# Order of a normalising product, engine of two relus and shape of one weight load in a fused attention and gated-FFN kernel

## The chip, the cores and the metric

The kernel runs on one core of a Trainium2 chip. The metric is device time in microseconds (us) of one execution; lower is better. Where I say "the profile" of a kernel, it is one execution of it taken by the hardware profiler; each kernel has one.

## The reference, cut to what matters

```python
def _attn_ref(q, k, v, n_global, n_local):      # 4 batches, 8 heads, 768 positions, head size 64
    scores = scale * q @ k.T - slope * dist     # ALiBi bias, causal window of 96 and 8 global keys
    a = softmax(where(keep, scores, -1e9))
    return a @ v

def _moe_ref(x, w_gate, w_val, w_out):          # x: 3072 tokens x 512; inner width 1536
    return (relu(x @ w_gate) * (x @ w_val)) @ w_out
```

## The kernel before

Tokens are worked off in eight halves of 384. While TensorE does the FFN of one half, the attention of the next is woven in, in small pieces. In the FFN, a *gate* group is four matmuls whose sum lies in one bank of PSUM, the memory into which TensorE writes; a relu reads it and frees the bank. A *value* group is four more in another bank; VectorE multiplies it with the relu's result, which gives `ht` and frees that bank. Three banks go round:

```python
P["ff"] = ctx.enter_context(tc.tile_pool(name="ffps", bufs=3, space=bass.MemoryType.PSUM, ...))

def gate(fc):
    psg = P["ff"].tile([128, 512], FP32, name="ff_ps")
    ...                                              # four matmuls into psg
    if fc in by_vector:                              # two groups of the first half only
        nc.vector.tensor_scalar_max(gr, psg[:, 0:QH], 0.0)
    else:
        nc.scalar.activation(gr, psg[:, 0:QH], AF.Relu, bias=0.0, scale=1.0)

def val(fc):
    psv = P["ff"].tile([128, 512], FP32, name="ff_ps")
    ...                                              # four matmuls into psv
    nc.vector.tensor_tensor(ht[:, fc, :], psv[:, 0:QH], st[fc], op=ALU.mult)
```

The attention of a pair of heads ends with a logarithm and an exponential on ScalarE (together the reciprocal of the softmax sum) and with two products on VectorE, one per head, that normalise into `xT`, the input of the next FFN:

```python
if e == 1:                                           # second head of the pair
    nc.scalar.activation(rc, ln, AF.Exp, bias=0.0, scale=-1.0)
    for e_ in range(2):
        r = slice(64 * e_, 64 * e_ + 64)
        nc.vector.tensor_tensor(xT_of[s][r, p, :], av_of[s, p, e_][r, 0:QH], rc[r], op=ALU.mult)
```

Pieces and FFN groups are put in order by `weave`; each engine then executes its own instructions in that order. In the text, x0 and x1 are the two heads' products, "es" the mask products of the attention, and ht5 and ht6 are the two `ht` products near them. I count value groups from 0 to 95 over the program.

At the start, GpSimd issues the loads: the gate weights come as three transfers of 512 columns, and behind the first of them comes q and k of the second half:

```python
def load_gate(i):
    load_w(wg[i], moe_w_gate, i * GW * 128, (i + 1) * GW * 128)      # GW = 4
...
f1_0[0][1]()                 # the first two gate groups, ahead of the second half's attention
```

The softmax here doesn't subtract the row's maximum and nothing guards it: scores larger than these inputs give would overflow.

## Time and profile before

| | before |
|---|---|
| median of the first three runs | 253.26 us (252.5 to 254.62) |
| median of all six runs beside the changed kernel | 252.68 us (252.4 to 254.62) |
| span of the profiled execution | 251.0 us |
| TensorE busy, share of the span | 96% |
| stalls ahead of gate and value groups in the five later passes | 2.33 us |

A later pass is one half's FFN with the next half's attention woven in, some 28 us. Stalls are counted from start to start: a matmul of 384 columns takes 0.16 us, and what a step takes beyond that is a stall.

### The profile page before, as it was taken

Reading aid. Unit: us, or ns where it says so; the run is one execution under the profiler, and the core shown is the slowest. Engines: PE = TensorE matmul, PEld = TensorE weight load, DVE = VectorE, ACT = ScalarE, POOL = GpSimd, SP = SyncE. Lnnn points to the kernel's source line nnn. Section 1 sums busy time; section 2 is a strip of 40 time slices with the busy share of each in tenths; the row PEclk is TensorE's granted clock in tenths of the full one; section 3 lists DMA queues with packets and bytes.
Section 4 is the critical chain, followed back from the end, with each engine's and each line's share of the span. In section 5 each row is a group of like instructions: output and inputs, shape, how many; then the busy total and the mean of one; then the engine's idle time right before and its main releaser. Section 6 shows DMA issues by size and latency. Waiting matters only on the chain.

```text
span 251.0 us, 4966 instructions
## 1 busy us (share of the span) xinstructions
PE 240.0 (96%) x1779; PEld 141.9 (57%) x1789; DVE 133.6 (53%) x346; ACT 156.4 (62%) x316; POOL 94.0 (37%) x213
## 2 busy tenths in 40 slices
PE   7969999999999999999999999999999999999994
PEld 3646555556555666556664566556565566556543
DVE  3744854775465657527662557527662657524410
ACT  6878755337675787557774687557774687553312
POOL 7988929700557326803437066302440000000000
PEclk9999999999999999999999999999999999999999
DMA  6999999992799993978349956829541100020012
GB/s 189 150 180 159 182 200 103 142 178 56 246 138 257 159 222 90 126 136 267 83 108 89 252 149 158 59 103 274 87 105 58 70 0 1 3 102 24 0 44 84
DMA packets 77705, 31.57 MB, mean 126 GB/s; under 512 B 57585, under 2 KB 74737, under 8 KB 77681
## 3 DMA queue, kind: packets, MB, share of 16 engines
q0 software_dynamic: 36208, 9.48, 38.4%
q1 hardware_dynamic: 41472, 21.78, 33.1%
q8 instruction: 14, 0.23, 0.4%
q14 instruction: 11, 0.08, 0.1%
HBM read 28.38 MB, written 6.29 MB: 138 GB/s over the span
## 4 chain that ended last, share of the span: by engine, by line
PE 78%; DVE 6%; ACT 5%; DMA 4%; POOL 4%; issue 2%; POOLq 0%; ACTq 0%; DVEq 0%
PE ff_ps L545 24%; PE ff_ps L524 21%; PE ff_ps L511 21%; PE av_ps L423 5%; PE qk_ps L395 4%; DMA qs<-in_q_dram 3%; DVE ht L526 2%; DVE xT L440 2%; POOL vbuf L169 1%; PE av_ps L299 1%; ACT grelu L517 1%; ACT rcp L437 1%; ACT lnd L432 1%; ACT es L376 1%; DMA out_dram<-osb 1%
## 5 line engine op out<-in xcount | busy, mean ns | idle before, releaser
L524 PE MATMUL ff_ps<-xT,wv 128*128 128x384 bf16 x384 | 78.1, 326 | 1.4 <-DVE ht L526 0.4
L511 PE MATMUL ff_ps<-xT,wg 128*128 128x384 bf16 x376 | 76.5, 326 | 0.4 <-DVE ht L526 0.2
L517 ACT ACTIVATE grelu<-ff_ps 128x384 bf16<-128x384 f32 x92 | 45.0, 489 | 34.3 <-PE ff_ps L511 18.3
L526 DVE TENSOR_TENSOR ht<-ff_ps,grelu 128x384 bf16<-128x384 f32 x96 | 53.4, 557 | 23.5 <-PE ff_ps L524 17.9
L545 PE MATMUL ff_ps<-wo_sb,ht 128*128 128x512 bf16 x267 | 63.9, 379 | 0.5
L440 DVE TENSOR_TENSOR xT<-av_ps,rcp 64x384 bf16<-64x384 f32 x48 | 26.6, 555 | 44.8 <-ACT rcp L437 41.9
L524 PEld LDWEIGHTS <-wv 128*128 128x128 bf16 x384 | 36.1, 97 | 24.4 <-issue 3.2
L511 PEld LDWEIGHTS <-wg 128*128 128x128 bf16 x376 | 35.0, 97 | 23.0 <-issue 1.1
L407 DVE TENSOR_TENSOR es<-es,m_all 128x432 bf16<-128x432 bf16 (+5 forms) x108 | 33.1, 334 | 22.6 <-ACT es L398 22.1
L398 ACT ACTIVATE es<-qk_ps 128x432 bf16<-128x432 f32 (+2 forms) x72 | 37.9, 528 | 10.1 <-PE qk_ps L395 8.2
L545 PEld LDWEIGHTS <-ht 128*128 128x128 bf16 x276 | 25.8, 97 | 26.8
L313 POOL CAST kc<-ks 128x384 bf16<-128x384 f32 x20 | 10.0, 540 | 60.5 <-DMA ks<-in_k_dram 60.5
L432 ACT ACTIVATE lnd<-av_ps 64x384 f32<-64x384 f32 x48 | 23.3, 485 | 11.7 <-PE av_ps L423 11.0
L550 ACT COPY osb<-ff_ps 128x512 f32<-128x512 f32 x23 | 13.5, 585 | 23.3 <-PE ff_ps L545 22.5
L169 POOL DMA_DIRECT2D vbuf<-in_v_dram x28 | 24.3, 878 | 1.5 <-DMA qs<-in_q_dram 1.0
L395 PE MATMUL qk_ps<-qT,kT 128*128 128x432 bf16 (+5 forms) x108 | 24.8, 286 | 0.0
L423 PEld LDWEIGHTS <-vbuf 128*128 128x128 bf16 x216 | 18.0, 98 | 7.4
L423 PE MATMUL av_ps<-es,vbuf 128*128 128x216 bf16 (+4 forms) x216 | 21.0, 226 | 0.0
L395 PEld LDWEIGHTS <-kT 128*128 128x128 bf16 x108 | 10.6, 98 | 7.6
L321 POOL CAST qz<-qs 128x192 bf16<-128x192 f32 x40 | 12.6, 362 | 2.1 <-DMA qs<-in_q_dram 1.8
L437 ACT ACTIVATE rcp<-lnd 128x384 f32<-128x384 f32 x24 | 12.5, 522 | 0.8
L376 ACT ACTIVATE es<-qk_ps 128x864 bf16<-128x864 f32 (+3 forms) x16 | 10.4, 709 | 1.0 <-PE qk_ps L371 0.8
(85 smaller groups left out, 153.6 us busy)
## 6 DMA issues: line engine op xcount, KB each, us to landing
out_dram<-osb SPq DMA_DIRECT2D x23, 256.0 KB
ks<-in_k_dram SPq DMA_DIRECT2D x5, 768.0 KB
qs<-in_q_dram SPq DMA_DIRECT2D x5, 768.0 KB
vbuf<-in_v_dram POOLq DMA_DIRECT2D x24, 120.0 KB, 4.2
wg<-in_moe_w_gate_dram POOLq DMA_DIRECT2D x3, 512.0 KB, 7.5
wv<-in_moe_w_val_dram POOLq DMA_DIRECT2D x3, 512.0 KB, 9.3
wo_sb<-in_moe_w_out_dram POOLq DMA_DIRECT2D x1, 1536.0 KB, 12.5
ks<-in_k_dram SPq DMA_DIRECT2D x4, 192.0 KB
```

What stands on the lines that cost most here:

```text
L169: nc.gpsimd.dma_start(out=v_dst(b, NG + r0, NG + r0 + n, j), in_=v[b, :, KT * j + r0 : KT * j + r0 + n, :].rearrange("h p d -> p h d"))
L395: nc.tensor.matmul(ps[:, c : c + n_], lhsT=kt[:, j, :], rhs=qd[:, :, :, a : a + w], start=True, stop=True)
L398: nc.scalar.activation(es[:, 0:cols], ps[:, 0:cols], AF.Exp, bias=0.0, scale=scale)
L407: nc.vector.tensor_mul(e4, e4, mk)
L423: nc.tensor.matmul(av3[:, :, a : a + w], lhsT=vb[:, j, z0 : z0 + 128], rhs=es[:, c : c + NN * w].rearrange("k (n p) -> k n p", n=NN), star ...
L432: nc.scalar.activation(ln[o0 : o0 + 64], av[d0 : d0 + 64, 0:QH], AF.Ln, bias=0.0, scale=1.0)
L440: nc.vector.tensor_tensor(xT_of[s][r, p, :], av_of[s, p, e_][r, 0:QH], rc[r], op=ALU.mult)
L511: nc.tensor.matmul(psg[:, 0:QH], lhsT=w_of(wg, dc, fc), rhs=xT[:, dc, :], start=(dc == 0), stop=(dc == N_DC - 1))
L517: nc.scalar.activation(gr, psg[:, 0:QH], AF.Relu, bias=0.0, scale=1.0)
L524: nc.tensor.matmul(psv[:, 0:QH], lhsT=w_of(wv, dc, fc), rhs=xT[:, dc, :], start=(dc == 0), stop=(dc == N_DC - 1))
L526: nc.vector.tensor_tensor(ht[:, fc, :], psv[:, 0:QH], st[fc], op=ALU.mult)
L545: nc.tensor.matmul(ps2, lhsT=ht[:, fc, n * 128 : (n + 1) * 128], rhs=wo_sb[:, fc, :], start=(fc == 0), stop=(fc == N_FC - 1))
```

## The change

Its intent: after a reciprocal, an `ht` product that gives back a PSUM bank should not stand behind both heads' products; two relus should leave VectorE; and the first gates should start on half of the first gate columns, with the third gate group moved ahead of the second half's attention to fill the wait for q.

```diff
+    def load_first_gate():
+        for f0 in (0, GW * 64):
+            load_w(wg[0][:, :, f0 : f0 + GW * 64], moe_w_gate, f0, f0 + GW * 64)
...
-            for e_ in range(2):
-                r = slice(64 * e_, 64 * e_ + 64)
-                nc.vector.tensor_tensor(xT_of[s][r, p, :], av_of[s, p, e_][r, 0:QH], rc[r], op=ALU.mult)
+            av_of[s, p, "r"] = rc
+    def piece_x(s, p, e):
+        r = slice(64 * e, 64 * e + 64)
+        nc.vector.tensor_tensor(xT_of[s][r, p, :], av_of[s, p, e][r, 0:QH], av_of[s, p, "r"][r], op=ALU.mult)
...
-            return (T(0) + BI(0, 0, 1) + T(1) + f[8] + SC(0, 0, 1) + f[9] + T(2) + ...
+            return (T(0) + BI(0, 0, 1) + T(1) + SC(0, 0, 1) + f[8] + T(2) + ...
...
+        def with_x(item, p, e):                 # x0 in the piece that ends the pair, x1 in the next
+            return (item[0], lambda: (item[1](), piece_x(s, p, e)))
+        for p, at in ((0, 7), (1, 12), (2, 16), (3, 20)):
+            for e in range(2):
+                order[at + e] = with_x(order[at + e], p, e)
...
-            if fc in by_vector:
-                nc.vector.tensor_scalar_max(gr, psg[:, 0:QH], 0.0)
-            else:
-                nc.scalar.activation(gr, psg[:, 0:QH], AF.Relu, bias=0.0, scale=1.0)
+            nc.scalar.activation(gr, psg[:, 0:QH], AF.Relu, bias=0.0, scale=1.0)
...
     f1_0[0][1]()
+    f1_0[4][1]()                                # third gate group
```

More of the change, by code (lines that the diff above doesn't have):

```diff
@@ L437, in piece_av @@
             nc.scalar.activation(rc, ln, AF.Exp, bias=0.0, scale=-1.0)
-            for e_ in range(2):
-                r = slice(64 * e_, 64 * e_ + 64)
-                nc.vector.tensor_tensor(xT_of[s][r, p, :], av_of[s, p, e_][r, 0:QH], rc[r],
-                                        op=ALU.mult)
+            av_of[s, p, "r"] = rc
+    def piece_x(s, p, e):
+        r = slice(64 * e, 64 * e + 64)
+        nc.vector.tensor_tensor(xT_of[s][r, p, :], av_of[s, p, e][r, 0:QH], av_of[s, p, "r"][r], op=ALU.mult)
     def piece_av_wide(s, p):
@@ L479, in attention_pieces @@
             return (C(0) + X(lambda: load_v_globals(0), lambda: load_v(0, 0), lambda: load_v(0, 1),
-                             lambda: load_v(0, 2), lambda: load_v(0, 3), lambda: load_gate(0),
+                             lambda: load_v(0, 2), lambda: load_v(0, 3), load_first_gate,
                              lambda: load_qk_cast(1, 0, 2), lambda: load_qk_cast(1, 2, 4))
@@ L489, in attention_pieces @@
             f = [[x] for x in fill]
-            return (T(0) + BI(0, 0, 1) + T(1) + f[8] + SC(0, 0, 1) + f[9] + T(2) + BI(1, 0) + SC(1, 0) + BI(1, 1) + SC(1, 1)
+            return (T(0) + BI(0, 0, 1) + T(1) + SC(0, 0, 1) + f[8] + T(2) + BI(1, 0) + SC(1, 0) + BI(1, 1) + SC(1, 1)
                     + T(3) + SC(2, 0, 1) + f[0] + SC(3, 0) + f[1] + SC(3, 1) + f[2] + AW(0) + f[3] + AW(1) + f[4]
@@ L495, in attention_pieces, with ffn_pieces @@
         a = AV(2)
-        return (QK(0) + QK(1) + AV(0) + QK(2) + AV(1) + g[0:1] + a[0:1] + g[1:2] + a[1:2] + g[2:3]
-                + [(0.0, lambda: None)] * 2 + AV(3))
+        order = (QK(0) + QK(1) + AV(0) + QK(2) + AV(1) + g[0:1] + a[0:1] + g[1:2] + a[1:2] + g[2:3]
+                 + [(0.0, lambda: None)] + AV(3) + [(0.0, lambda: None)])
+        def with_x(item, p, e):
[3 more added lines that the diff above has]
+                order[at + e] = with_x(order[at + e], p, e)
+        return order
     out_v = out.rearrange("(s p n) d -> s n p d", p=128, n=NN)
-    def ffn_pieces(c, by_vector=()):
+    def ffn_pieces(c, pair_gates=False):
         ht = ht_pool.tile([128, N_FC, QH], BF16, name="ht")
@@ L566, in ffn_pieces @@
         f1 = []
-        if by_vector:
+        if pair_gates:
             f1 = [(0.65, two_gates), (0.65, lambda: val(0)), (0.0, lambda: None), (0.65, lambda: val(1))]
@@ L624 @@
     load_w(wo_sb, moe_w_out, 0, DM)
-    f1_0, f2_0 = ffn_pieces(0, range(GW, 2 * GW - 2))
+    f1_0, f2_0 = ffn_pieces(0, True)
     f1_1, f2_1 = ffn_pieces(1)
@@ L629 @@
     f1_0[0][1]()
+    f1_0[4][1]()
     for h in range(4, H):
         mask(h)
-    for _, f in attention_pieces(1, [f1_0[i] for i in (1, 3, 5, 7, 8, 10, 9, 11, 4, 6)]):
+    for _, f in attention_pieces(1, [f1_0[i] for i in (1, 3, 5, 7, 8, 10, 9, 11, 6)]):
         f()
```

## The prediction

> **What bounds the kernel now.** I read the page's busy shares first, then the busy time by stretches, then the waits of TensorE alone, then the chain of waits and the timeline where those waits lie.
>
> ```profile
> PE 240.0 (96%) x1779; PEld 141.9 (57%) x1789; DVE 133.6 (53%) x346; ACT 156.4 (62%) x316; POOL 94.0 (37%) x213
> ...
> 0.00:36.00 36.00, 30.33 (x397) 18.96 (x399) 21.28 (x70) 25.46 (x51) 29.08 (x58) 1.00 1.27 176
> ...
> 82.00:110.90 28.90, 28.46 (x193) 16.91 (x192) 16.70 (x41) 19.63 (x39) 12.52 (x30) 1.00 0.98 153
> 110.90:138.90 28.00, 27.73 (x182) 16.31 (x180) 15.41 (x36) 18.96 (x39) 11.72 (x29) 1.00 0.68 133
> ...
> PE ff_ps L560 <- DMA wg<-in_moe_w_gate_dram: 1.1, 1, 1.1
> PE av_ps L299 <- DMA qs<-in_q_dram: 1.0, 1, 1.0
> ...
> PE ff_ps L524 <- DVE grelu L515: 0.4, 1, 0.4
> ```
>
> The second to fourth lines are stretches (length, then busy time of TensorE matmul, weight load, VectorE, ScalarE, GpSimd). TensorE is the bound: 5.7 us of its 11 us of idleness lie in the first 36 us, and each later pass of about 28 us leaves 0.3 to 0.4 us. So nothing in this change can be worth much. TensorE's own work doesn't change; only its waits can. Busy time hides part of a wait, since the ends of matmuls are modelled. So I took the steps from start to start: four 128x384 matmuls take 0.65 us, that is 0.1625 us each, and what a step has beyond its own columns at that rate is a stall. Sums of this kind: 1.23 us ahead of the first gates (16.84), 1.13 us ahead of the second tile's transposes (19.27), five small ones from 25 to 40 us (0.31, 0.28, 0.53, 0.28, 0.24), and in the five passes with attention from 82 us on 0.72, 0.38, 0.54, 0.38, 0.31 us, 2.33 us together, all of them released by the product on L526.
>
> ```profile
> 9.67 0.80 POOL wg L186
> 10.46 0.69 POOL qs L145
> 11.15 8.07 DMA qs<-in_q_dram
> 19.23 0.04 issue
> 19.27 0.53 PE av_ps L299 x12
> ...
> 16.84 1.47 PE L560 MATMUL ff_ps<-xT,wg 128*128 128x384 bf16 x8 [1.05 <-DMA wg<-in_moe_w_gate_dram]
> 19.27 0.53 PE L299 MATMUL av_ps<-ident,qs 128*64 128x128 bf16 x12 [0.96 <-DMA qs<-in_q_dram]
> ```
>
> The chain passes through the gate load's issue and the q load behind it, not through the first gates: TensorE waits at 16.84 for the gate columns, but then waits again for q. Making the first wait shorter gains nothing unless work is moved into the second.
>
> ```profile
> 92.34 1.14 DVE L440 TENSOR_TENSOR xT<-av_ps,rcp 64x384 bf16<-64x384 f32 x2 [1.96 <-ACT rcp L437]
> 93.51 0.56 DVE L526 TENSOR_TENSOR ht<-ff_ps,grelu 128x384 bf16<-128x384 f32 x1
> 93.99 0.86 DVE L407 TENSOR_TENSOR es<-es,m_all 128x144 bf16<-128x144 bf16 x2
> 94.77 0.55 DVE L526 TENSOR_TENSOR ht<-ff_ps,grelu 128x384 bf16<-128x384 f32 x1
> ...
> 94.12 0.81 PE L524 MATMUL ff_ps<-xT,wv 128*128 128x384 bf16 x4
> ...
> 95.37 0.48 PE L511 MATMUL ff_ps<-xT,wg 128*128 128x384 bf16 x2 [0.25 <-DVE ht L526]
> ```
>
> VectorE sits idle 1.96 us behind the reciprocal, does both heads' products, and only then the product ht that gives a PSUM bank back. Call it ht5, and the next ht6. The value matmuls at 94.12 wait for ht5 (0.30 us), the gate at 95.37 for ht6 (0.42 us).
>
> **What the Trainium skill says.** "TensorE: Matmul & The Clock Gate", Architectural detail: ScalarE and VectorE take their queues strictly in order. The trace agrees: ht5's matmuls ended by 91.6, and it starts at 93.51, after both products. "VectorE: DVE Perf Modes", Two Vector instructions with no wait between them: an instruction whose inputs or output start in another group of 32 partitions than the one before is held until all earlier ones have finished. The trace agrees: the second head (partitions 64 up) starts 31 ns after the first has ended, ht5 32 ns after the second, while unheld neighbours start 80 ns before the end of the one before (0.474 us from ht5 to the es product, against 0.558 us long). "DMA: Bandwidth & Descriptors", Why a DMA increments its semaphore by 16 and not by 1: a load has landed only when all 16 engines have posted. In the trace's semaphore records 15 engines had posted the gate by 16.20 and the last at 16.79; for q of the first two heads it is 17.31 and 19.23. The slow engine also carried a 16 KB instruction fetch of 0.95 us from 17.02. "ScalarE: Activation LUTs", Rules for kernel authors, advises VectorE for a relu. Here, from PSUM, the trace has 548 ns on VectorE and 489 ns on ScalarE, so the move costs nothing.
>
> **The change part by part.**
>
> *Gate load in two.* One transfer of 1024-byte rows becomes two of 512-byte ones. At full rate the packet records show some 200 packets of 1024 bytes a microsecond and 480 of 384 bytes over 16 engines, so 80 and 33 ns an engine; on a straight line 512 bytes take 43 ns. An engine's 32 packets of 80 ns (2.56 us) become 64 of 43 (2.73 us): everything behind them in the queue lands about 0.2 us later, the q load at about 19.4 in place of 19.23. GpSimd pays one more issue, 0.8 us, which hides: the first k load is issued at 10.45 while its first packets move at 14.5. The first half lands, on the slowest engine, near 15 (half of its 12.86 to 16.79). TensorE is free at 15.8, so the first gates then wait for the last xT product, which ends at 17.21. They finish near 17.6 in place of 18.15. By itself that is worth nothing, for q still comes at 19.4.
>
> *Third gate moved ahead of the second tile.* This is what fills the hole. It needs a PSUM bank of the first gates, free after their relu at about 18.05, runs 18.1 to 18.75, and is done before q lands. The step that it leaves, between the transposes and the first scores, was 0.76 us (20.97 to 21.72 in the chain). From the transposes on, TensorE is therefore 0.76 - 0.2 = 0.55 us ahead. ScalarE follows: masks end near 21.2, and the first exponentials, now from 22.25, can start at about 21.4. The weights land early enough: the first value columns at 24.7 (+0.2) against use at 25.8 - 0.55, the second at 32.1 (+0.2) against 33.25 - 0.55.
>
> *Two relus to ScalarE.* The 0.53 us stall at 34.43 waits for the relu that VectorE ends at 34.39, behind a product. On ScalarE the first relu goes between the 0.52 us reciprocal that ends at 32.14 and the next logarithm, and the second follows 32.14 + 0.49 (relu) + 0.49 (ln) + 0.52 (exp) + 0.49, with issue gaps about 34.2. Gain 0.2 us. The 0.28 us stall at 37.49, behind a ScalarE relu, stays.
>
> *Second head's product one piece later.* The code spreads 22 pieces over 0.88 of 23.4 us, one per 0.94 us, between FFN groups of 0.65 us. Around the first pair the VectorE order is now x0, x1, ht5, es, es, ht6; it becomes x0, ht5, es, es, x1, ht6. So ht5 ends at 92.34 + 0.47 + 0.56 = 93.4 in place of 94.07, and the stall at 94.12 goes. But x1 still stands before ht6. VectorE is busy without a gap from 92.34 on, and there are two held starts before and after (x1 and ht5; then x1 and ht6). So ht6 still ends at about 95.3, and the gate at 95.37 waits for it just as long: 0.30 us is handed to the next wait. In the second kind of pass ht6 ends at 123.53 and the gate starts at 123.62, so some 0.05 us are won. Over five passes: about 0.1 us of the 2.33.
>
> That is so if the gate keeps the bank which ht6 frees. The bank freed by the relu at 94.02 is ready at 94.51. If the new order makes the allocation take that one, the waits vanish and all 2.33 us come back. In the kernel before, at this place the rotation already deviates: the gate at 93.17 waits for ScalarE and the value after it for VectorE, the reverse of the usual. I give this one chance in five.
>
> Sum: 0.55 + 0.2 + 0.1 = 0.85 us likely, 0.85 + 2.2 = 3.0 us at best; weighted 0.8 x 0.85 + 0.2 x 3.0 = 1.3 us. 253.26 - 1.3 = 252.0.
>
> **The rivals.** *The split delays q by more.* If 512-byte packets cost far more than the line says, or the instruction fetch and the slow engine add up worse, q lands 0.8 us later and eats the moved gate: gain 0.3 us or less, 253.0. For it: the slow engine is already 1.9 us behind the others at q. Against: the fetch is on that engine's path in both kernels. *All bank waits vanish*: about 250.3. For it: VectorE is 53% busy and idles 1.96 us just ahead. Against: the idle time lies before the burst, and the burst's length is unchanged. *Holding a PSUM bank longer hurts*: the second head's accumulator is released a piece later; but two more pieces pass before its next use, so I see no loss. *ScalarE becomes the bound*: 0.98 us more of 156.4 at 62%, no.
>
> **Range and chances.** Runs of the kernel before spread 252.5 to 254.62, so about 1 us is noise. The cases give 250.3 to 253.0; with noise 250.3 to 253.4. A gain of over 2% would need 5.1 us, most of the 6.3 us of all the stalls named above at once (1.23 + 1.13 + 1.64 + 2.33); a loss of that size has no source.
>
> **What would show it.** The first gates start near 15.8; the third gate's four matmuls lie before the second tile's transposes; those start at 19.3 to 19.7; no wait on a VectorE relu; x1 after the es products; the value matmuls near 93.5 no longer wait, and the gate two groups on still waits for L526 (or doesn't, in the rival with another bank). I am wrong if transposes start after 20.0, if all L526 waits are gone, or if a new wait appears after 36 us.

## More of the kernel before

The lines are in the prediction. One more, of the groups by line, is of use later. Its columns are line, engine, operation, tiles, shapes, count, then busy time and mean ns of one, then the engine's idle time ahead of the group and what ended most of it:

```profile
L440 DVE TENSOR_TENSOR xT<-av_ps,rcp 64x384 bf16<-64x384 f32 x48 | 26.6, 555 | 44.8 <-ACT rcp L437 41.9
```

VectorE idles 44.8 us in front of these products, nearly all of it for ScalarE's reciprocal: whatever stands behind the products in VectorE's queue waits with them.

## The result, and the profile after

The changed kernel took 250.12 us (median of six runs, 249.38 to 250.52) against 252.68 us. The ratio is 0.9885, with a 95% interval of 0.9854 to 0.9915. A ratio here is the mean time of one kernel's runs over that of the other's of the same rounds, so not quite the ratio of the medians. That is 1.2% faster: below the predicted range of 250.3 to 253.4 us.

To see where the time went I lined up the starts of the 96 value groups in the two profiles. TensorE's lead over the kernel before:

| value group (time before) | lead, us | what lies between |
|---|---|---|
| 0 (25.8 us) | 0.32 | start |
| 6 to 16 (36.6 to 52 us) | 0.87 | the two relus: +0.55 |
| 18 to 22 (55 to 61 us) | 0.26 | a new stall at 54 us: -0.61 |
| 24 (82.7 us) | 0.15 | -0.11, not traced |
| 32 | 0.86 | first later pass: +0.71 |
| 44 | 1.24 | second: +0.38 |
| 56 | 1.76 | third: +0.52 |
| 68 | 2.14 | fourth: +0.38 |
| 80 to 95 | 2.46 | fifth: +0.32 |

The steps sum to 0.32 + 0.55 - 0.61 - 0.11 + 2.31 = 2.46 us, and the spans differ by 251.0 - 248.5 = 2.5 us. The five passes gave all their stalls back; I had predicted 0.1 us there.

First the page's busy shares and groups of the profile after, then stretches of it (start:end, length, then busy time of TensorE matmul, weight load, VectorE, ScalarE and GpSimd, the granted clock, DMA share and GB/s):

```profile
PE 240.5 (97%) x1789; PEld 142.7 (57%) x1789; DVE 133.8 (54%) x344; ACT 157.2 (63%) x318; POOL 94.8 (38%) x214
...
L447 DVE TENSOR_TENSOR xT<-av_ps,rcp 64x384 bf16<-64x384 f32 x48 | 26.6, 555 | 35.2 <-ACT rcp L442 23.4
```

```profile
36.00:62.00 26.00, 25.43 (x190) 14.72 (x188) 16.83 (x45) 12.43 (x27) 10.76 (x17) 1.00 1.03 120
...
82.00:110.00 28.00, 28.00 (x193) 16.84 (x191) 16.37 (x40) 19.55 (x39) 12.26 (x30) 1.00 1.01 158
110.00:137.60 27.60, 27.60 (x182) 16.34 (x180) 15.57 (x36) 18.96 (x39) 11.73 (x29) 1.00 0.67 133
```

No engine does noticeably more or less work, and the products cost the same 555 ns each. But the idle time ahead of the products that is put down to the reciprocal has fallen from 41.9 to 23.4 us: work that stood behind both products now stands behind one. (It is not saved. The page puts 11.0 us ahead of the products down to the output matmuls, 2.2 us before, and VectorE's wait for ScalarE's es has grown from 22.1 to 30.1 us.) And in the passes from 82 us on TensorE is busy without a hole (28.00 of 28.00 us, 27.60 of 27.60 us). The stretch from 36 to 62 us, by contrast, has 0.57 us without work; that is the new stall.

The waits of TensorE (engine, tile and line, what it waited for, us in total, times, longest):

```profile
PE qk_ps L376 <- DVE kT L284: 0.7, 1, 0.7
PE ff_ps L523 <- ACT grelu L573: 0.4, 1, 0.4
PE ff_ps L523 <- DVE ht L535: 0.4, 1, 0.4
```

The line on the VectorE relu is gone. One wait on `ht` is left, and it is not in a later pass: it is the new one at 54 us. The second line is the moved third gate, waiting for the relu of the first gates.

Now the place from the prediction, 92 to 96 us, on VectorE and then on TensorE:

```profile
92.19 0.55 DVE L447 TENSOR_TENSOR xT<-av_ps,rcp 64x384 bf16<-64x384 f32 x1 [1.96 <-ACT rcp L442]
92.66 0.54 DVE L535 TENSOR_TENSOR ht<-ff_ps,grelu 128x384 bf16<-128x384 f32 x1
93.14 0.98 DVE L412 TENSOR_TENSOR es<-es,m_all 128x144 bf16<-128x144 bf16 x2
94.16 0.56 DVE L447 TENSOR_TENSOR xT<-av_ps,rcp 64x384 bf16<-64x384 f32 x1
94.75 0.56 DVE L535 TENSOR_TENSOR ht<-ff_ps,grelu 128x384 bf16<-128x384 f32 x1
```

```profile
93.67 0.81 PE L533 MATMUL ff_ps<-xT,wv 128*128 128x384 bf16 x4
...
94.50 0.81 PE L523 MATMUL ff_ps<-xT,wg 128*128 128x384 bf16 x4
```

The order is x0, ht5, es, es, x1, ht6, as predicted. ht5 ends at 93.20, so the value group at 93.67 doesn't wait. ht6 ends at 94.75 + 0.56 = 95.31, where I had said "about 95.3". Yet the gate group starts at 94.50, 0.8 us *before* ht6 ends. So it cannot be using the bank that ht6 frees.

The compiled programs say why. They list for each FFN tile its PSUM bank and the engine whose work its first matmul waits for. Around this gate (tile 70 in order of allocation, counted from 0; g and v are gate and value):

```
        before                      after
68 g    bank 6, waits for ScalarE   bank 6, waits for ScalarE
69 v    bank 7, waits for VectorE   bank 7, waits for VectorE
70 g    bank 5, waits for VectorE   bank 6, waits for ScalarE
71 v    bank 6, waits for ScalarE   bank 5, waits for VectorE
```

With the new order of instructions, tiles 70 and 71 have changed places: the gate got the bank that a relu on ScalarE frees, the value group after it the one that ht6 frees, and the value group comes 0.96 us later, at 95.46. Why the allocation picks so was not looked into; that it does is plain from the listing.

### The profile page after: what moved, and what is told of

It is laid out like the page before. It is cut to its first block, busy times and chain, and to the rows that moved or that the text cites. A ratio compares the mean times of both kernels' runs of the same rounds, so it can differ in the third digit from the quotient of the medians.

```text
span 248.5 us, 4970 instructions
## 1 busy us (share of the span) xinstructions
PE 240.5 (97%) x1789; PEld 142.7 (57%) x1789; DVE 133.8 (54%) x344; ACT 157.2 (63%) x318; POOL 94.8 (38%) x214
## 4 chain that ended last, share of the span: by engine, by line
PE 80%; DMA 8%; POOL 4%; DVE 3%; ACT 3%; issue 1%; SPq 1%; ACTq 0%; POOLq 0%
PE ff_ps L554 24%; PE ff_ps L523 21%; PE ff_ps L533 20%; PE av_ps L428 6%; PE qk_ps L400 5%; DMA wv<-in_moe_w_val_dram 5%; DMA qs<-in_q_dram 2%; POOL vbuf L169 1%; DVE qT L314 1%; PE qk_ps L358 1%; PE qk_ps L376 1%; DVE kT L282 1%; DMA out_dram<-osb 1%; POOL vbuf L174 1%; ACT lnd L469 1%
## 5 line engine op out<-in xcount | busy, mean ns | idle before, releaser
L526 ACT ACTIVATE grelu<-ff_ps 128x384 bf16<-128x384 f32 x94 | 45.9, 489 | 33.8 <-PE ff_ps L523 17.7
L535 DVE TENSOR_TENSOR ht<-ff_ps,grelu 128x384 bf16<-128x384 f32 x96 | 54.2, 566 | 22.5 <-PE ff_ps L533 19.0
L412 DVE TENSOR_TENSOR es<-es,m_all 128x432 bf16<-128x432 bf16 (+5 forms) x108 | 33.6, 339 | 30.4 <-ACT es L403 30.1
L447 DVE TENSOR_TENSOR xT<-av_ps,rcp 64x384 bf16<-64x384 f32 x48 | 26.6, 555 | 35.2 <-ACT rcp L442 23.4
L428 PE MATMUL av_ps<-es,vbuf 128*128 128x216 bf16 (+4 forms) x216 | 20.4, 226 | 0.0
```

The costliest lines, as they stand in the source:

```text
L412: nc.vector.tensor_mul(e4, e4, mk)
L428: nc.tensor.matmul(av3[:, :, a : a + w], lhsT=vb[:, j, z0 : z0 + 128], rhs=es[:, c : c + NN * w].rearrange("k (n p) -> k n p", n=NN), star ...
L447: nc.vector.tensor_tensor(xT_of[s][r, p, :], av_of[s, p, e][r, 0:QH], av_of[s, p, "r"][r], op=ALU.mult)
```

## The experiments

My theory after reading the result (A): the bank swap, which comes with the product's move, gives the five passes; the product's new place alone or the new banks alone would not. Rivals: (B) the order alone is enough, because VectorE has room; (C) the banks alone are enough; (D) the relus or the start gave a part of it. All kernels gave correct results.

### The parts of the change alone

**The product's move alone:**

```diff
-            for e_ in range(2):
...
-                nc.vector.tensor_tensor(xT_of[s][r, p, :], av_of[s, p, e_][r, 0:QH], rc[r], op=ALU.mult)
+            av_of[s, p, "r"] = rc            # and piece_x, with_x and the new order as in the change
```

> Only the second head's product is moved. Theory A (the passes' gain comes from the moved product together with the new PSUM bank that the allocation gives the gate behind it): the five stalls behind L526 in the passes vanish, 2.3 us, so about 250.4 where the kernel before has 252.7 (ratio 0.991), and no new stall near 54 us, since the start is not shifted. Rival B (my prediction as it stood, with the bank unchanged): 0.1 us, 252.6. Rival C (the gain is mostly the start's): under 1 us, above 251.7.

It took 251.05 us (250.31 to 251.72) against 252.87 us, ratio 0.9932 (0.991 to 0.9955), that is 1.7 us less, though I had expected 2.3; the reason comes below. In its profile no gate or value group of the later passes stalls, and the lead gained there is 2.30 us. Its compiled program has the changed kernel's bank map.

**The start's two parts alone:**

```diff
-                             lambda: load_v(0, 2), lambda: load_v(0, 3), lambda: load_gate(0),
+                             lambda: load_v(0, 2), lambda: load_v(0, 3), load_first_gate,
...
     f1_0[0][1]()
+    f1_0[4][1]()                            # and the list of fill pieces without it
```

> Only the gate load in two and the third gate moved ahead; relus and product as before. If the trace of the changed kernel reads true: TensorE is 0.3 us ahead from the second tile's scores on, perhaps less than 0.3 us of it lost again near 47 us where GpSimd's memset lengthens a VectorE copy; so 0.0 to 0.3 us in all, 252.4 to 252.7. My prediction had 0.55 us for it: 252.1.

253.07 us (252.6 to 253.52), ratio 1.0016 (0.9996 to 1.0036): worth nothing. I had expected 252.4 to 252.7 us.

**The relus alone:**

```diff
-            if fc in by_vector:
-                nc.vector.tensor_scalar_max(gr, psg[:, 0:QH], 0.0)
-            else:
-                nc.scalar.activation(gr, psg[:, 0:QH], AF.Relu, bias=0.0, scale=1.0)
+            nc.scalar.activation(gr, psg[:, 0:QH], AF.Relu, bias=0.0, scale=1.0)
```

> Only the two relus go to ScalarE. The trace of the changed kernel shows 0.55 us won between 25 and 36 us; my prediction had 0.2 us. Theory D (a lead at 45 us runs into GpSimd's memset and is mostly lost): 0.0 to 0.3 us in all, 252.4 to 252.7, with the stall in the trace near 47 to 55 us. Without D: 252.1 to 252.2.

252.92 us (251.56 to 254.53), ratio 1.0005 (0.997 to 1.0039). By time alone nothing can be told. The stall near 54 us that I had expected did not come either. The trace tells what the relus are worth: from value group 0 to value group 10 TensorE took 16.49 us in the kernel before and in the start-only kernel, and 15.95 us here, 0.54 us less. This stretch lies behind the start and ahead of everything else that was changed.

I had predicted 0.2 us, with the second relu ending near 34.2. ScalarE of the relus-only kernel:

```profile
31.51 0.52 ACT L465 ACTIVATE rcp<-lnd 128x384 f32<-128x384 f32 x1
31.94 0.47 ACT L514 ACTIVATE grelu<-ff_ps 128x384 bf16<-128x384 f32 x1
32.31 0.48 ACT L463 ACTIVATE lnd<-av_ps 128x384 f32<-128x384 f32 x1
32.82 0.52 ACT L465 ACTIVATE rcp<-lnd 128x384 f32<-128x384 f32 x1
33.25 0.47 ACT L514 ACTIVATE grelu<-ff_ps 128x384 bf16<-128x384 f32 x1
```

The relu that follows a reciprocal starts 0.43 us after it, though the reciprocal is 0.52 us long, and the logarithm starts 0.37 us after a relu of 0.47 us. Neighbours overlap by 0.09 to 0.10 us, and I had added up full durations. The Trainium skill has this, in "ScalarE: Activation LUTs", What ACT_TABLE_LOAD costs: back-to-back instructions of this kind overlap by about 93 ns. I had not read that line. The second relu ended at 33.72, before TensorE came to the group that needs it, at 33.78. Of the 0.53 us stall only 0.09 us is left, as at most changes from one kind of group to another here; the remaining 0.11 us was won at the value group before, which had waited for the first relu.

### Order and banks apart

The banks are chosen by the allocation, so to separate them from the order I dealt them by hand: three pools of one bank each in place of one pool of three, and a list, read from the *other* kernel's compiled program, that says which pool the n-th tile takes. As a check I dealt each original its own map; its compiled waits were the original's without a difference. With the other kernel's map ten waits change, all of them on TensorE: in each of the five passes one gate and one value group exchange what they wait for, ScalarE or VectorE. Nothing else in the program differs.

```diff
-        P["ff"] = ctx.enter_context(tc.tile_pool(name="ffps", bufs=3, ...))
+        banks = [ctx.enter_context(tc.tile_pool(name=f"ffps{i}", bufs=1, ...)) for i in range(3)]
+        P["ff"] = Given(banks)              # serves the n-th tile from banks[BANKS[n]]
```

**The changed kernel with the banks of the kernel before:**

> The changed kernel, with every PSUM bank of the FFN tiles given by hand as the kernel before has it; nothing else differs. Theory A: the gate two groups behind the product waits for ht6 again, which ends no sooner than before, so the passes win only 0.1 us in place of 2.3: 252.2 to 252.5. Rival E (the moved product is enough, whichever bank): 250.1 as the changed kernel.

252.45 us (251.97 to 253.0), ratio 0.9995 (0.9974 to 1.0017). Its VectorE, TensorE and waits:

```profile
94.08 0.56 DVE L553 TENSOR_TENSOR ht<-ff_ps,grelu 128x384 bf16<-128x384 f32 x1
```

```profile
93.50 0.81 PE L551 MATMUL ff_ps<-xT,wv 128*128 128x384 bf16 x4
94.69 0.81 PE L541 MATMUL ff_ps<-xT,wg 128*128 128x384 bf16 x4 [0.19 <-DVE ht L553]
...
PE ff_ps L541 <- DVE ht L553: 1.1, 5, 0.3
```

The value group at 93.50 no longer waits; the gate at 94.69 starts 0.05 us after ht6 has ended at 94.64, and so it goes in all five passes. This is the prediction's picture to the letter: the wait is handed from the value group to the gate.

**The kernel before with the banks of the changed kernel** (the same edit, on the kernel before):

> The kernel before, with every PSUM bank of the FFN tiles given by hand as the changed kernel has it; the product order stays old. Theory A (order and bank are needed together): the value matmuls still wait for ht5 behind both products (0.30, 0.38, 0.30, 0.38, 0.31 us, 1.7 in all), but the gate behind no longer waits for ht6 (0.42 and 0.23 us won): 0.65 us, 252.2. Rival F (the bank is the whole cause): 2.3 us, 250.5. Rival G (neither matters by itself): 252.8.

252.61 us (252.13 to 254.17), ratio 0.9997 (0.9955 to 1.0039).

```profile
93.42 0.56 DVE L544 TENSOR_TENSOR ht<-ff_ps,grelu 128x384 bf16<-128x384 f32 x1
```

```profile
94.03 0.81 PE L542 MATMUL ff_ps<-xT,wv 128*128 128x384 bf16 x4
94.86 0.81 PE L529 MATMUL ff_ps<-xT,wg 128*128 128x384 bf16 x4
```

Here the value group at 94.03 still waits for ht5, which ends at 93.98 behind both products. The gate does not wait for ht6.

Counted in all profiles, the stalls over 60 ns ahead of gate and value groups in the later passes are:

| | banks of before | banks of after |
|---|---|---|
| products together (old order) | five value stalls, 1.68 us; in one of three profiles two gate stalls of 0.65 us more | five value stalls, 1.67 us |
| second product later (new order) | five gate stalls, 1.89 us | none (changed kernel, run again, product alone, product and relus; also four of the five kernels with moved memsets told of below, the fifth has one of 0.09 us) |

Theory A holds, B and C fall: each half alone removes nothing that counts, both together remove everything. The old bank map needs ht6 early and the old order makes ht5 late; only together do they let both go.

The top left cell also corrects a reading of mine. I had taken all 2.33 us of the kernel before as there in every execution. In the start-only and relus-only kernels, which have its order and its banks, the two gate stalls (0.42 us ahead of the gate at 95.37, and 0.23 us in the third pass) are missing, and the five value stalls of 1.68 us remain (with one of 0.07 us elsewhere in the first). What makes the difference is the pair of es products that stands between ht5 and ht6. In the kernel before it took 0.67 us in the third pass against 0.47 in the start-only kernel; in the first pass it is the 0.86 us of the prediction's timeline, and beside it ran a cast on GpSimd:

```profile
92.80 1.86 POOL L313 CAST kc<-ks 128x384 bf16<-128x384 f32 x4 [8.75 <-DMA ks<-in_k_dram]
```

In the start-only kernel that cast ended at 94.33, and the same pair took 0.47 us:

```profile
94.47 0.47 DVE L412 TENSOR_TENSOR es<-es,m_all 128x144 bf16<-128x144 bf16 x2
```

The cast starts when its k load has landed, so its place shifts from execution to execution. The lasting part of the passes is thus about 1.7 us, and that is what the product-alone kernel was timed at (1.7 us, interval 1.1 to 2.3). In the changed kernel's timeline above, the pair beside the cast took even 0.98 us and nothing stalled: with the new banks it is a later group that waits for ht6. This slack is not endless: in one kernel with moved memsets (below) the pair took 1.13 us, and a gate stalled by 0.09 us.

### The run again, and the stall at 54 us

**The changed kernel once more, unedited**, to see what differs between executions:

```diff
 (no edit)
```

> The changed kernel once more, beside the three that follow, so that they can be compared on one chip. 249.8 to 250.6. In its trace the transposes of the third tile come near 45 us again; if the lead over the kernel before is then over 0.8 us, VectorE's key copy meets GpSimd's memset and TensorE loses about 0.6 us near 54; with a smaller lead it loses nothing (in the runs so far: 0.87 lost, 0.65 and 0.41 not).

250.42 us (250.16 to 250.99) against 253.03 us, ratio 0.9896 (0.9862 to 0.9931). The later passes gave 2.30 us again; the stall at 54 us had shrunk to 0.11 us.

The cause of that stall lies seven microseconds earlier. GpSimd and VectorE, in the kernel before and then in the changed one:

```profile
45.64 2.73 POOL L639 MEMSET qz<- 128x1536 uint32 x2
47.59 0.82 DVE L279 COPY kT<-kT 128x56 bf16<-128x56 bf16 x1
```

```profile
45.89 2.72 POOL L649 MEMSET qz<- 128x1536 uint32 x2
46.72 1.92 DVE L284 COPY kT<-kT 128x56 bf16<-128x56 bf16 x1
...
54.04 0.81 PE L523 MATMUL ff_ps<-xT,wg 128*128 128x384 bf16 x4 [0.39 <-DVE ht L535]
```

The copy moves 56 columns from SBUF to SBUF and takes 0.18 us elsewhere. The memsets end at 48.37 and 48.61, and the copies at 48.41 and 48.64: 0.03 to 0.04 us after them. That was so in each of the seven profiles where the copy fell beside the memsets, and where it came after their end (the product-alone and start-only kernels) it took 0.18 us. The copies from PSUM just ahead of it, beside the same memsets, kept their 0.53 and 0.17 us. The Trainium skill explains it in "SBUF — State Buffer", SBUF: two separate sides: VectorE and GpSimd share a pair of ports which is "an exclusive lock, not a bandwidth split". It holds this for a GpSimd instruction against, among others, a VectorE instruction in a mode that uses both of its ports. The trace agrees in what waits and until when; the mode of the copy it does not show.

The changed kernel is 0.87 us ahead at this point, so its VectorE reaches the copy 0.83 us after the beginning of the memsets, where the kernel before reached it after 1.95 us, and it is shut out longest. Everything behind it on VectorE is late, the transposes' copies there are packed without a gap, and the delay comes out as a stall at 54 us. The stall against the copy's length is 0.56 for 1.92 us, 0.37 for 1.68 (the product-and-relus kernel, below) and 0.11 for 1.42: each time the copy less 1.31 to 1.36 us, which is the slack there. Shorter copies made none.

**The memsets moved** some 15 us ahead (to 29.5 and 33.0 us), between loads of the third half:

```diff
     for p in range(HP):
         load_qk_cast(2, 2 * p, 2 * p + 2)
+        if p in (1, 2):
+            nc.gpsimd.memset(qz[2 - p]..., 0)
...
-    for i in range(2):
-        nc.gpsimd.memset(qz[1 - i]..., 0)
```

> The changed kernel with GpSimd's two long memsets of qz moved ahead, into time in which GpSimd waits for loads (31 to 38 us). If the memset is what lengthened VectorE's key copy from 0.18 to 1.92 us, the copy takes 0.18 us in the trace, the stall near 54 is gone, and the time is 0.0 to 0.6 us under the changed kernel's, by how many of its executions run into it. If something else held the copy, it stays over 1 us.

249.81 us (249.59 to 250.18), ratio 0.9872 (0.9834 to 0.9909). The copy is back at its size and the stall is gone:

```profile
47.26 0.18 DVE L284 COPY kT<-kT 128x56 bf16<-128x56 bf16 x1
```

**Product and relus without the start's parts:**

```diff
     (the product's move and the relus of the change, as above; load_gate(0) and f1_0[4] as before)
```

> Moved product and relus on ScalarE, with the gate load whole and the third gate in its old place. By theory: 2.3 + 0.55 us less than the kernel before, 249.9 to 250.3, as fast as the changed kernel, since the gate load in two and the earlier third gate are worth nothing on average (start_only ran at 1.0016 of the kernel before). If these were worth the 0.3 to 0.55 us that the first trace and my prediction give, it is 250.4 to 250.7, behind the changed kernel.

250.54 us (250.39 to 250.76), ratio 0.9901 (0.9867 to 0.9935), as good as the whole change within the error. The time lies in the range that I had given the case in which the start's parts count, but the changed kernel took 250.42 us in the same set of runs, so it was not behind. So rival D holds for the relus (0.54 us) and not for the start.

### The start's parts, with the memsets moved

Four kernels, all with product, relus and moved memsets, one for each combination of the first gate load (whole or in two) and the third gate (old place or moved). Their edits against the moved-memset kernel:

```diff
 memset_split_moved: none (the same kernel again)
 memset_whole_moved, memset_whole_old:
-                             lambda: load_v(0, 2), lambda: load_v(0, 3), load_first_gate,
+                             lambda: load_v(0, 2), lambda: load_v(0, 3), lambda: load_gate(0),
 memset_split_old, memset_whole_old:
-    f1_0[4][1]()
+    # back in the second half's list, behind its second transposes
```

> The changed kernel with the memsets moved ahead, again (the reference of the three that follow: gate load in two, third gate ahead of the second tile's transposes). 249.6 to 250.2.

> The same with the gate load whole again. Theory H (the first gates mostly wait for the last xT product, which ends at 18.0 to 19.2 in all profiles but the first, so the early half is rarely used): within 0.3 us of the reference, and the first gates start 0 to 1 us later in its trace. If the split is worth its 0.5 us: 250.2 to 250.7.

> The same with the gate load in two, but the third gate behind the transposes as in the kernel before. Theory H: within 0.3 us of the reference, since the third gate ahead of the transposes waits 0.58 us for its bank and delays them (20.2 in place of about 19.3) by about what it saves behind them (0.67 us). If moving the gate fills an empty hole: 0.5 us slower, 250.2 to 250.7.

> Both start parts undone: moved product, relus on ScalarE, memsets ahead. Theory H: within 0.3 us of the reference, 249.6 to 250.4. If the two start parts together are worth my prediction's 0.55 us: 250.2 to 250.9.

| | median (lowest to highest), us | ratio (95%) |
|---|---|---|
| in two, moved | 250.47 (249.28 to 250.58) | 0.9901 (0.9877 to 0.9925) |
| whole, moved | 250.33 (250.12 to 250.63) | 0.9908 (0.9889 to 0.9927) |
| in two, old place | 249.85 (249.13 to 250.49) | 0.9886 (0.9864 to 0.9908) |
| whole, old place | 250.15 (249.55 to 252.01) | 0.9907 (0.9877 to 0.9937) |

All the intervals overlap, and no combination is shown to be better. I had expected all four within 0.3 us of the first; the third is 0.6 us below it, which may hint that moving the gate costs something. The moved-memset kernel, at 249.81 us in one set of runs, was at 250.47 us in the next, on another chip. So I name no version that beats the changed kernel.

Why the start's parts are worth nothing shows in the chain of the changed kernel (start, duration, what):

```profile
18.42 0.50 ACT grelu L573
...
18.97 0.81 PE ff_ps L523 x4
19.78 0.46 PE av_ps L304 x12
```

The third gate was to run in the hole ahead of q. It needs a bank of the first gates, their relu ends at 18.92, and so it starts at 18.97. It takes 0.65 us from start to start, and so the transposes behind it start at 19.71, though q had landed at 19.52. In the six other profiles with the gate moved q landed at 18.1 to 18.7, ahead of the gate's start at 19.4 to 19.7: there was no hole for it to fill. The first gates themselves are late because the last xT product ended at 18.01 (predicted 17.21): in most profiles that product, not the weights, came last. In six of the seven profiles with the gate moved the transposes start 1.70 us after that product's end, and in the seventh 1.89 us.

All fourteen profiles together show what the move is worth. From the first of these transposes to value group 0 it is 6.54 us in each of the seven with the gate in its old place, and 5.78 us in each of the seven with the gate moved: the 0.76 us of the prediction is saved. But the transposes start at 19.36 us on average with the old place (18.90 to 19.99) and at 20.23 us with the gate moved (19.71 to 20.45), so 0.87 us is lost ahead of them. Value group 0 starts at 25.90 us on average with the old place and at 26.01 with the gate moved, no difference beside the spread. One kernel's profile and another's differ by up to 1.1 us there (25.44 to 26.53). When the very first loads land (8.2 to 9.3 us) does not explain it, for the profile in which they came latest has the earliest value group 0; why the last xT product ends anywhere from 17.21 to 19.20 us was not traced.

## Why the prediction was wrong, and where it was right

- **What bounds the kernel:** right. TensorE stayed the bound, and only stalls were won.
- **Gate load in two:** right that it is worth nothing by itself. The 43 ns for a packet of 512 bytes was too low: counted in the same way, the changed kernel starts at most 314 such packets in a microsecond, which is 51 ns on each of 16 engines. The first half landed at 15.19 ("near 15") and q at 19.52 ("about 19.4"), but that q agrees means little: in most other kernels with the load in two it landed at 18.1 to 18.9, so the 0.2 us that I had worked out are lost in the spread between executions. That the instruction fetch lay on the engine that was last with q is an inference: the kept trace shows the fetch (16 KB, 0.95 us from 17.02) but not its engine.
- **Third gate ahead:** wrong in size. "TensorE is therefore 0.76 - 0.2 = 0.55 us ahead" became 0.32 us in this one profile and nothing on average. The 0.76 us was right; the 0.2 us that the transposes were to lose was 0.44 us in this profile and 0.87 us on average, and "those start at 19.3 to 19.7" came out as 19.71 to 20.45, in six of seven profiles after 20.0, which I had named as a sign of being wrong. The path to the transposes leads through the last xT product, the first gates, their relu and the moved gate, and not through q. The gate was to run from 18.1; it ran from 18.97, because the relu that frees its bank came 0.9 us later than I had it from the kernel before, whose last xT product, at 17.21, is the earliest of all fourteen profiles (the others: 17.8 to 19.2).
- **Relus:** mechanism right, size wrong: 0.2 predicted, 0.54 to 0.55 measured. The term at fault is "32.14 + 0.49 (relu) + 0.49 (ln) + 0.52 (exp) + 0.49": it adds whole durations, and the starts follow each other 0.37 to 0.43 us apart where nothing else is waited for.
- **The product, the step that failed:** "So ht6 still ends at about 95.3, and the gate at 95.37 waits for it just as long: 0.30 us is handed to the next wait", and from it "Over five passes: about 0.1 us of the 2.33". The first half came true: ht6 ended at 95.31, and with the old banks the gate does wait for it, in all five passes (1.89 us in all). But it was bound to "if the gate keeps the bank which ht6 frees", to which I gave four chances in five, and it didn't. The rival that I named, the bank freed by the relu, was what happened; all 2.33 us vanished from the trace, of which about 1.7 us were lasting. I did see that the rotation deviates at this very place, and still weighed the case as unlikely: the rotation was taken as fixed although the order of the instructions that feed it was being changed.
- **Not foreseen:** the stall at 54 us, 0.61 us in this profile. I had named a new wait after 36 us as a sign of being wrong but had no cause for it.

In sum, the likely case was 0.55 + 0.2 + 0.1 = 0.85 us, and the profiles gave 0.32 + 0.55 + 2.31 - 0.61 - 0.11 = 2.46 us. The rival's "about 250.3" for the case that all bank waits vanish lies 0.2 us from the measured 250.12, and that is partly luck. It takes 3.0 us from 253.26, the median of three runs; beside the changed kernel the kernel before was at 252.68, so the gain was 2.56 us. In it the start gave less than predicted and the relus more, and the new stall took 0.6 us away again.

## What to carry to other kernels

Which buffer a tile gets is part of a change of order: before saying which wait remains, find out whose release the next tile will wait for, for moving an instruction can re-deal the buffers. Sort the stalls of one profile into lasting and accidental ones by looking at several profiles of the same code; here 0.65 of 2.33 us were accidental. And an engine that gets ahead meets other neighbours: look for long memsets or casts on GpSimd that it will now run into.

## What the Trainium skill lacked or had wrong

- "ScalarE: Activation LUTs", Rules for kernel authors: the advice to give relus to VectorE gives its figure for the fast bf16 mode and doesn't tell a PSUM source apart. From PSUM, 128x384, a relu took 489 ns on ScalarE and 548 ns on VectorE, and the two that were moved gained 0.54 us. The same page's overlap of about 93 ns was right (0.09 to 0.10 us here) and stands where one looking for durations misses it.
- "SBUF — State Buffer", SBUF: two separate sides: it says that the lock is held for the whole instruction. Here it outlasted one: the 1.92 us copy started while the first of two memsets in a row still ran and ended 0.03 us after the second (whose record begins 0.09 us before the first's end), so a waiting VectorE copy did not get in between the two. The page gives no such case and no figure for a memset; here a copy of 0.18 us took 0.54 to 1.92 us.
- The same section, on two SBUF inputs beside a GpSimd instruction that reads SBUF: agreed with, but without a size. A pair of es products took 0.47 to 0.48 us alone, in all fourteen profiles, and between 0.47 and 1.13 us beside GpSimd's casts.
- No page has what an instruction fetch costs the data loads: each profile has a 16 KB fetch of 0.95 to 0.98 us between 15.8 and 18.1 us. In the kernel before, the last DMA engine was 0.7 us behind the fifteen others with the load that landed at 17.45, and 1.9 us with q, the next one, after the fetch had begun at 17.02. That the fetch caused it is likely and not shown, as the trace doesn't name its engine.
